# First four attention chunks: loads in order of need, and the next chunk's scores issued ahead of the current chunk's other products

## The chip, the cores and the metric

One core of one Trainium2 chip runs the whole program. The metric is the device time of one execution in microseconds (us). Of the kernel before there are three timed runs, 1011.18, 1013.14 and 1015.83 us; the median is 1013.14 us.

## The reference

Three layers follow one another on B=4 sequences of S=768 tokens with H=8 heads of D=48 channels (model width 384).

```python
# 1. a recurrence over the tokens of each head (state is 48 x 48)
cur   = (u * k_t) outer v_t
y_t   = r_t @ (state + cur)
state = w_t[:, None] * state + k_t outer v_t
# 2. an MLP: x is (3072, 384), w_in (384, 2048), w_out (2048, 384)
h = x @ w_in;  g = where(h > 0, h, exp(min(h, 0)) - 1);  x = g @ w_out
# 3. a second MLP of the same shape with g = h * sigmoid(1.702 h)
```

## The kernel before

**The recurrence by chunks.** The tokens are taken in 24 chunks of 128 (six to a sequence). For chunk c the host lays out `w` (decays), `kr` (keys and queries, 112 partitions, four pairs of heads) and `tok` (128 tokens x r, k, v). The steps, with the engine that does each:

- `decay` (VectorE, L240 to L249): two scans, the running product of w (`e`) and its inverse (`gi`), each in one buffer.
- `queries` (L278, `r` = queries times `e`), `keys` (L270, `kh` = keys times `gi`), `weigh` (L330, L331, q·k·u per token) on GpSimd, unless another engine is named.
- `bonus`: VectorE sums `weigh` per head (L341), then GpSimd multiplies v by the sum (L343, `qv`).
- `block` (ScalarE, L290): copies `r` into the block-diagonal `blk`, one buffer.
- `scores_pe` (TensorE): 4 products of `kh` with `blk` into the PSUM tile `pa`, then 4 transposes of `kh` into `pk`. `scores`: two masked copies of `pa` into the one tile `at` (VectorE, L375), and a copy of `pk` to `kt` (ScalarE, L378).
- `y_pe` (TensorE): `at` times v, and `r` times the state. `y` (VectorE, L397) adds `qv`.
- `state_pe` (TensorE), then `state` (VectorE, L417 to L420): the new state `s`.
- `x_pe` (TensorE): transposes y. `xt` (ScalarE L431, VectorE L432): splits it into a high and a low part, the MLP's input.

**The MLPs.** Tokens are taken in 6 tiles of 512 (4 chunks), the hidden width in 16 slices f. Products are in split precision: w and x each as high and low part, three passes. A slice's weights arrive as int words (`raw`) and are rebuilt by three VectorE operations (L97, then L107 twice: "bits"), split by a ScalarE cast (L132) and a VectorE subtraction (L133: "parts"). A step computes `h` (L143, 9 products), the activation (L154 to L156 in layer 1), its split (L166, L167) and the second product (L174). Steps of layer 1's first tile rebuild the weights of slice j+2 as they go. From chunk 4 on, the recurrence's steps are woven into the MLP's steps.

**What sets the order.** Nothing is reordered: each engine runs its instructions in the order in which the program issues them, and waits are put in for data and for buffers. All loads go through one queue (SyncE). Chunks 0 to 3 have no MLP step to run beside: the function `lead` writes out their order. The changed part of the order is all in `lead`: in the loop over c it issues `y_pe(c)`, `state_pe(c)`, `scores_pe(c+1)` and `x_pe(c)`, prepares `decay`, `keys`, `queries`, `block` of chunk c+2, and takes slices of weight work (`take`) beside them. `warm` issues bf16 products on constant data that nothing reads (L353). At its end the first weight slices are ready, and the MLP starts.

Of the kernel before, what the change touches and what calls it, by code (L numbers as in the profile page):

```python
# [12 lines left out]
F32 = mybir.dt.float32  # L13
# [9 lines left out]
B, H, S, D = 4, 8, 768, 48  # L23
P = 128
C = 128
NCB = S // C
NCH = B * NCB
NP = H // 2
PR = 112
HALF = ((0, 48), (64, 112))  # L30
NT = B * S
DM = H * D
# [19 lines left out]
class Moe:  # L52
# [33 lines left out]
    large = small = None  # L86
# [106 lines left out]
class Attention:  # L193
# [79 lines left out]
    def queries(self, c, engine=None):  # L273
        if c >= NCH or "r" in self.t[c]:
            return
        nc, t = self.nc, self.t[c]
        r = t["r"] = self.p.tile([PR, NP, C], F32, tag="r", name="r", bufs=2)
        (engine or nc.gpsimd).tensor_tensor(out=r, in0=t["kr"][:, NP * C:].rearrange("p (s t) -> p s t", t=C),  # L278
                                            in1=t["e"][:, :, :C], op=ALU.mult)

# [27 lines left out]
    def verdict(self, bad):  # L308

        nc = self.nc  # L310
        large = self.p.tile([P, CHECKS], F32, tag="rk", name="large")
        s = self.p.tile([P, 2], F32, tag="q", name="s")
        nc.vector.tensor_scalar(out=large, in0=self.c["large"], scalar1=HIGH_LARGE, scalar2=0.0,
                                op0=ALU.is_lt, op1=ALU.is_equal)
        nc.vector.tensor_reduce(out=s[:, 0:1], in_=large, axis=AX.X, op=ALU.add)
        nc.vector.tensor_reduce(out=s[:, 1:2], in_=self.c["flag"], axis=AX.X, op=ALU.add)
        pb = self.ps.tile([P, H, C], F32, tag="a", name="pb", bufs=1)[:, 0, :]
        for i in range(2):
            nc.tensor.matmul(pb[:1, :1], self.c["one"], s[:, i:i + 1], start=i == 0, stop=i == 1)
        nc.vector.tensor_scalar(out=bad, in0=pb[:1, :1], scalar1=0.0, scalar2=None, op0=ALU.not_equal)  # L320

    def weigh(self, c, engine=None):

        if c >= NCH or "rk" in self.t[c]:
            return
        nc, t = self.nc, self.t[c]
        tok = t["tok"]
        rk = t["rk"] = self.p.tile([P, DM], F32, tag="rk", name="rk")
        engine = engine or nc.gpsimd
        engine.tensor_tensor(out=rk, in0=tok[:, :DM], in1=tok[:, DM:2 * DM], op=ALU.mult)  # L330
        engine.tensor_tensor(out=rk, in0=rk, in1=self.c["u"], op=ALU.mult)  # L331
# [23 lines left out]
    def scores_pe(self, c):  # L355
        nc, t = self.nc, self.t[c]
        kh, blk = t["kh"], t["blk"]
        pa = t["pa"] = self.ps.tile([P, H, C], F32, tag="a", name="pa", bufs=1)
        if "khl" in t:
            mm = [partial(nc.tensor.matmul, pa[:, 2 * p:2 * p + 2, :], t["khl"][:, a, p, :], blk[:, b, p, :, :],  # L360
                          start=i == 0, stop=i == len(PASSES) - 1) for p in range(NP) for i, (a, b) in enumerate(PASSES)]
        else:
            mm = [partial(nc.tensor.matmul, pa[:, 2 * p:2 * p + 2, :], kh[:, p, :], blk[:, p, :, :],
                          start=True, stop=True) for p in range(NP)]
        if not self.last(c):
            pk = t["pk"] = self.psum("pk")
            mm += [partial(nc.tensor.transpose, pk[:, p * PR:(p + 1) * PR], kh[:, p, :], self.c["ident"][:PR, :PR])
                   for p in range(NP)]
        return mm

    def scores(self, c):
        nc, t, at = self.nc, self.t[c], self.c["at"]
        m = self.c["mask"].unsqueeze(1).to_broadcast([P, NP, C])
        for j in range(2):
            nc.vector.copy_predicated(at[:, NP * j:NP * (j + 1), :], m, t["pa"][:, NP * j:NP * (j + 1), :])  # L375
        if not self.last(c):
            kt = t["kt"] = self.p.tile([P, NP * PR], F32, tag="kt", name="kt", bufs=2)
            nc.scalar.copy(kt, t["pk"][:, :NP * PR])  # L378
# [14 lines left out]

    def y(self, c):
        nc, t = self.nc, self.t[c]
        x = t["x"] = self.p.tile([P, DM], F32, tag="x", name="x")
        nc.vector.tensor_tensor(out=x, in0=t["qv"].rearrange("p h d -> p (h d)"), in1=t["py"][:, :DM], op=ALU.add)  # L397

    def state_pe(self, c):
# [42 lines left out]
def issue(a, b, late=0):  # L442

    for f in a[:late]:
        f()
    a, done = a[late:], 0
    for i, f in enumerate(a):
        f()
        while done < len(b) and (done + 1) * len(a) <= (i + 1) * len(b) + len(a) // 2:
            b[done]()  # L450
            done += 1
    for f in b[done:]:
        f()
# [4 lines left out]
LATE = (0, 6, 2, 6)  # L458


MADE, BITS = (0, 0, 1, 2), (0, 3, 7, 8)
WARM = (11, 4, 2)
AHEAD = MADE[-1]
NTILE = NT // TILE
STEPS = 2 * NTILE * NF
CHECKS = 4 * NF
# [3 lines left out]
def layers(nc, moe, w1, w2, x2d, out, x_of, beside, lead):  # L470
# [66 lines left out]
    for j in range(STEPS):  # L537
# [10 lines left out]
        if j < turn:  # L548
            n = min(j + AHEAD + 1, NF)
            loads, squares, bits = min(n + 3, NF), min(n + 1, NF), 4 * n  # L550
# [70 lines left out]
def fast(tc, rkw, tok, u, w1, w2, out, bad, x2d):  # L621
    nc = tc.nc
    with ExitStack() as ctx:
# [6 lines left out]
        with tc.manual_schedule():  # L630
            moe = Moe(nc, pools, ps)
            c = {}
            at = Attention(nc, ap, c, ps, rkw, tok)
# [8 lines left out]
            per = TILE // C  # L642

            def xt(c):
                i, o = divmod(c, per)
                if i not in xts:
                    xts[i] = pools["xt"].tile([P, 2, KD, TILE], F32R, tag="xt", name="xt")
                at.xt(c, xts[i], o * C)
# [30 lines left out]
            first = 4 * per + 1  # L679

            def lead(take):
                at.load(0)
                at.load(1, 0)
                nc.sync.dma_start(at.c["u"], u.partition_broadcast(P))
                at.load_tok(0)
                at.load(1, 1)
                at.load(2, 0)
                take("load", 1)
                at.load(2, 1)
                at.load_tok(1)  # L690
                at.load_tok(2)
                at.load(3)
                at.load_tok(3)
                take("load", 2)
                at.load(4)
                at.decay(0)
                at.queries(0)
                at.keys(0, nc.vector)
                at.block(0, (nc.scalar.copy, nc.vector.tensor_copy))
                at.warm(WARM[0])  # L700
                issue(at.scores_pe(0), [])
                at.decay(1)
                at.queries(1)
                at.keys(1)
                at.scores(0)
                at.weigh(0, nc.vector)
                at.bonus(0)
                at.block(1)
                for c in range(per):
                    made = MADE[c]  # L710
                    at.warm(WARM[1])
                    issue(at.y_pe(c), [])
                    at.decay(c + 2)
                    at.bonus(c)
                    take("bits", BITS[c])
                    at.keys(c + 2)
                    at.queries(c + 2)
                    at.weigh(c + 1)
                    at.warm(WARM[2])
                    issue(at.state_pe(c), [])  # L720
                    at.y(c)
                    if c == per - 1:
                        issue(at.x_pe(c), [])
                    issue(at.scores_pe(c + 1), [])
                    at.state(c)
                    if c == per - 1:
                        xt(c)
                    at.scores(c + 1)
                    if c < per - 1:
                        issue(at.x_pe(c), [])  # L730
                        xt(c)
                    if c == 0:
                        take("load", 3)
                        at.load_tok(4)
                        at.load(5)
                        at.load_tok(5)
                    take("bits", 4 * made)
                    take("parts", made)
                    at.block(c + 2)
                take("load", 5)  # L740
                at.load(per + 2)
                at.bonus(per)
                at.alone = False

            def beside(j):
# [13 lines left out]
                return ([], 0, lambda: None, decays) if 0 <= k <= NCH and odd else NOTHING  # L759

            layers(nc, moe, w1, w2, x2d, out, xts.pop, beside, lead)


def any_decay(tc, wkr, vrow, up, w1, w2, out, x2d, xd):
# [48 lines left out]
    with ExitStack() as ctx:  # L813
# [12 lines left out]
        def lead(take):  # L826
            for k in range(AHEAD):
                for what, n in (("load", 1), ("sq", 1), ("bits", 4), ("parts", 1)):
                    take(what, n * (k + 1))
            take("load", AHEAD + 3)  # L830
            take("sq", AHEAD + 1)

# [55 lines left out]
```

## Time and profile before

| | |
|---|---|
| median of three runs | 1013.14 us |
| profiled execution: time / span | 1009.45 us / 1007.2 us |
| mean granted TensorE clock | 0.979 |
| busy: TensorE / VectorE / ScalarE / GpSimd | 966.6 / 707.3 / 459.6 / 179.5 us |
| chain that ended last: TensorE / VectorE | 78% / 14% |

The span is the profiled execution from the first to the last instruction; the 2.25 us around it are in the time and not in the span. In the rows further down, PE is TensorE (PEld its weight loads), DVE VectorE, ACT ScalarE, POOL GpSimd and SP SyncE. A timeline row reads: start in us, duration in us, engine, line, operation, out<-in, shapes, count; in brackets the idle time of the engine before it and what ended it. Rows of one line and engine close together are merged. L448 and L450 are the helper through which the products are issued; their tile names tell them apart.

### The profile page before, as it was taken

What the parts mean: (1) busy time and instruction counts of PE and PEld (TensorE: products, weight loads), DVE (VectorE), ACT (ScalarE), POOL (GpSimd) and SP (SyncE); (2) the same over time, 40 slices, a digit from 0 to 9 for tenths busy, and PEclk for the clock granted to TensorE, in tenths of its full rate; (3) what the DMA queues carried; (4) which work ended last, traced back from release to release, by engine and by line L of the source; (5) the groups of instructions that cost most, each with busy time, mean ns of one, the idle gap of its engine ahead of it and who ended that gap; (6) DMA issues with size and microseconds to landing.
All of it is one profiled execution on the core that took longest, in us unless ns stands there. A gap on an engine that the chain in (4) does not pass through costs nothing.

```text
span 1007.2 us, 13002 instructions
## 1 busy us (share of the span) xinstructions
PE 966.6 (96%) x4895; PEld 829.3 (82%) x4895; DVE 707.3 (70%) x1102; ACT 459.6 (46%) x886; POOL 179.5 (18%) x147
## 2 busy tenths in 40 slices
PE   7888889999999999999999999999999999999997
PEld 5677677788888878878888879999989899899896
DVE  7999997677667766776635888757666676676432
ACT  3243344444444445444445554446565565544322
POOL 5542323333323423423300000000000000000000
PEclk9798989999999999999999999999999999999999
DMA  9845401221211222212005560134353354432001
GB/s 239 231 176 177 146 28 51 86 72 52 83 51 51 61 83 71 74 45 90 1 1 193 195 216 25 41 119 135 122 181 123 119 180 124 142 116 79 32 1 35
DMA packets 35351, 101.89 MB, mean 101 GB/s; under 512 B 4048, under 2 KB 7248, under 8 KB 35280
## 3 DMA queue, kind: packets, MB, share of 16 engines
q1 hardware_dynamic: 35280, 100.98, 31.4%
q8 instruction: 40, 0.66, 0.3%
q14 instruction: 31, 0.25, 0.1%
HBM read 91.53 MB, written 9.44 MB: 100 GB/s over the span
## 4 chain that ended last, share of the span: by engine, by line
PE 78%; DVE 14%; issue 3%; POOL 2%; ACT 1%; DMA 0%; ACTq 0%; POOLq 0%; DVEq 0%
PE h L143 34%; PE o L183 20%; PE o L174 16%; DVE wt L107 4%; PE py L450 3%; PE pa L450 2%; DVE w L133 2%; DVE hl L167 1%; DVE wt L97 1%; DVE g L156 1%; PE pd L450 1%; DVE parts L294 1%; DVE e L240 1%; DVE gi L247 1%; ACT w L132 1%
## 5 line engine op out<-in xcount | busy, mean ns | idle before, releaser
L143 PE MATMUL h<-xt,w 128*128 128x512 f32 x1728 | 469.4, 401 | 4.2 <-DVE w L133 3.0
L143 PEld LDWEIGHTS h<-xt,w 128*128 128x128 f32 x1728 | 318.1, 189 | 66.5 <-DVE w L133 5.8
L174 PE MATMUL o<-hl,w 128*128 128x512 f32 x864 | 280.5, 428 | 6.1 <-DVE x L515 6.1
L183 PE MATMUL o<-w,hl 128*128 128x384 f32 x1152 | 217.8, 337 | 3.1 <-ACT e L159 2.1
L183 PEld LDWEIGHTS o<-w,hl 128*128 128x128 f32 x1152 | 204.4, 188 | 13.0 <-ACT e L159 3.3
L166 ACT CAST hl<-g 128x512 fp32r<-128x512 f32 x192 | 118.9, 619 | 188.4 <-DVE g L156 86.0
L174 PEld LDWEIGHTS o<-hl,w 128*128 128x128 f32 x864 | 158.5, 193 | 32.5 <-DVE x L515 7.5
L167 DVE TENSOR_TENSOR hl<-g,hl 128x512 fp32r<-128x512 f32 x192 | 150.2, 783 | 43.7 <-ACT hl L166 42.4
L156 DVE SCALAR_TENSOR_TENSOR g<-e,h 128x512 f32<-128x512 f32 x96 | 65.6, 683 | 68.1 <-ACT e L155 67.7
L160 DVE TENSOR_TENSOR g<-e,h 128x512 f32<-128x512 f32 x96 | 65.9, 686 | 66.5 <-ACT e L159 66.5
L159 ACT ACTIVATE e<-h 128x512 f32<-128x512 f32 x96 | 57.3, 597 | 101.0 <-PE h L143 101.0
L154 ACT ACTIVATE e<-h 128x512 f32<-128x512 f32 x96 | 57.3, 596 | 54.2 <-PE h L143 54.0
L450 PEld LDWEIGHTS py<-tok,at 128*128 128x128 f32 x304 | 60.4, 200 | 15.7 <-issue 4.4
L107 DVE SCALAR_TENSOR_TENSOR wt<-raw,wt 128x768 int32<-128x768 int32 x64 | 67.5, 1055 | 1.6
L155 ACT ACTIVATE e<-e 128x512 f32<-128x512 f32 x96 | 60.7, 632 | 3.1
L375 DVE COPY_PREDICATED at<-mask,pa 128x512 f32<-128x512 int32 x48 | 32.3, 726 | 38.6 <-PE pa L450 38.5
L270 POOL TENSOR_TENSOR kh<-kr,gi 112x512 f32<-112x512 f32 x19 | 31.6, 1661 | 150.1 <-issue 133.0
L450 PE MATMUL py<-tok,at 128*128 128x48 f32 x304 | 50.3, 248 | 6.2 <-issue 3.6
L450 PE MATMUL pa<-parts,khl 112*128 112x256 f32 x192 | 54.5, 284 | 1.0 <-DVE parts L294 1.0
L123 DVE TENSOR_SCALAR checked<-checked 128x384 f32<-128x384 f32 x64 | 22.8, 356 | 39.7 <-ACT checked L122 39.7
L378 ACT COPY kt<-pk 128x448 f32<-128x448 f32 x20 | 10.7, 534 | 86.2 <-PE pk L450 64.0
L132 ACT CAST w<-wt 128x768 fp32r<-128x768 f32 x32 | 26.7, 833 | 49.5 <-DVE wt L107 44.5
(111 smaller groups left out, 933.4 us busy)
## 6 DMA issues: line engine op xcount, KB each, us to landing
raw<-in_w SPq DMA_DIRECT2D x32, 768.0 KB, 4.5
seen<-in_w SPq DMA_DIRECT2D x64, 384.0 KB, 3.2
tok<-in_tok SPq DMA_DIRECT2D x20, 576.0 KB, 3.9
kr<-in_rkw SPq DMA_DIRECT2D x20, 448.0 KB, 3.6
seen<-in_rkw SPq DMA_DIRECT2D x24, 226.2 KB, 3.6
x2d<-x SPq DMA_DIRECT2D x18, 256.0 KB, 2.3
x<-x2d SPq DMA_DIRECT2D x18, 256.0 KB, 3.8
w<-in_rkw SPq DMA_DIRECT2D x20, 226.2 KB, 2.6
```

The costliest lines, as they stand in the source:

```text
L107: yield nc.vector.scalar_tensor_tensor(out=ti, in0=a, scalar=n, in1=ti, op0=shift, op1=put)
L143: nc.tensor.matmul(h[:, :n], w[:, a, k * P:(k + 1) * P], x[:, b, k, :n], start=i == 0, stop=i == len(mm) - 1)
L154: nc.scalar.activation(e[:, :n], h[:, :n], AF.Exp)
L155: nc.scalar.activation(e[:, :n], e[:, :n], AF.Relu, bias=1.0, scale=-1.0)
L156: nc.vector.scalar_tensor_tensor(out=g[:, :n], in0=e[:, :n], scalar=-1.0, in1=h[:, :n], op0=ALU.mult, op1=ALU.max)
L159: nc.scalar.activation(e[:, :n], h[:, :n], AF.Sigmoid, scale=1.702)
L160: nc.vector.tensor_tensor(out=g[:, :n], in0=e[:, :n], in1=h[:, :n], op=ALU.mult)
L166: nc.scalar.copy(hl[:, 0, :n], g[:, :n])
L167: nc.vector.tensor_tensor(out=hl[:, 1, :n], in0=g[:, :n], in1=hl[:, 0, :n].bitcast(F32), op=ALU.subtract)
L174: nc.tensor.matmul(acc[d][:, :n], w[:, a, DM + d * P:DM + (d + 1) * P], hl[:, b, :n], start=f == 0 and i == 0, stop=f == NF - 1 and i == 2)
L183: nc.tensor.matmul(acc[s][:, :DM], hl[:, b, s * P:(s + 1) * P], w[:, a, DM:2 * DM], start=f == 0 and i == 0, stop=f == NF - 1 and i == 2)
L450: b[done]()
```

## The change

The loads of chunks 0 to 2 come chunk by chunk. In the loop, `scores_pe(c+1)` is issued first, then `x_pe(c-1)`, `y_pe(c)`, `state_pe(c)`. So that scores of two chunks can be live at once, odd chunks put theirs into the two PSUM banks of tag `h`, and a third `r` buffer is added. `rk` (the result of `weigh`) and `x` lie in `tok` instead of tiles of their own. `queries(0)` moves from GpSimd to VectorE. The `warm` products in the loop are gone (those ahead of it stay). On VectorE, `xt` of the chunk before stands after `bonus`, the masked copies of the next chunk stand before `state`, and the weight work of `take` stands behind `block`, at c=2 and c=3 alone.

```diff
-        rk = t["rk"] = self.p.tile([P, DM], F32, tag="rk", name="rk")
+        rk = t["rk"] = tok[:, DM:2 * DM]
...
-        pa = t["pa"] = self.ps.tile([P, H, C], F32, tag="a", name="pa", bufs=1)
+        if self.alone and c % 2:
+            pa = [self.ps.tile([P, NP, C], F32, tag="h", name="pa", bufs=2) for _ in range(2)]
+        else:
+            pa = self.ps.tile([P, H, C], F32, tag="a", name="pa", bufs=1)
+            pa = [pa[:, :NP, :], pa[:, NP:, :]]
...
-        x = t["x"] = self.p.tile([P, DM], F32, tag="x", name="x")
+        x = t["x"] = t["tok"][:, :DM]
...
-MADE, BITS = (0, 0, 1, 2), (0, 3, 7, 8)
-WARM = (11, 4, 2)
+BITS = (0, 0, 4, 8)
+WARM = 11
...
             def lead(take):
-                at.load(0)
-                at.load(1, 0)
-                nc.sync.dma_start(at.c["u"], u.partition_broadcast(P))
-                at.load_tok(0)
-                at.load(1, 1)
-                at.load(2, 0)
+                for c in range(3):
+                    at.load(c)
+                    at.load_tok(c)
+                    if c == 0:
+                        nc.sync.dma_start(at.c["u"], u.partition_broadcast(P))
                 take("load", 1)
-                at.load(2, 1)
-                at.load_tok(1)
-                at.load_tok(2)
                 at.load(3)
...
-                at.queries(0)
+                at.queries(0, nc.vector)
...
                 at.scores(0)
+                at.block(1)
                 at.weigh(0, nc.vector)
-                at.bonus(0)
-                at.block(1)
                 for c in range(per):
-                    made = MADE[c]
-                    at.warm(WARM[1])
+                    issue(at.scores_pe(c + 1), [])
+                    if c > 0:
+                        issue(at.x_pe(c - 1), [])
                     issue(at.y_pe(c), [])
+                    issue(at.state_pe(c), [])
                     at.decay(c + 2)
                     at.bonus(c)
-                    take("bits", BITS[c])
+                    if c > 0:
+                        xt(c - 1)
                     at.keys(c + 2)
                     at.queries(c + 2)
                     at.weigh(c + 1)
-                    at.warm(WARM[2])
-                    issue(at.state_pe(c), [])
                     at.y(c)
-                    if c == per - 1:
-                        issue(at.x_pe(c), [])
-                    issue(at.scores_pe(c + 1), [])
+                    at.scores(c + 1)
                     at.state(c)
-                    if c == per - 1:
-                        xt(c)
-                    at.scores(c + 1)
-                    if c < per - 1:
-                        issue(at.x_pe(c), [])
-                        xt(c)
                     if c == 0:
+                        at.load_tok(4)
                         take("load", 3)
-                        at.load_tok(4)
                         at.load(5)
                         at.load_tok(5)
-                    take("bits", 4 * made)
-                    take("parts", made)
                     at.block(c + 2)
+                    take("bits", BITS[c])
+                    take("parts", BITS[c] // 4)
+                issue(at.x_pe(c), [])
+                xt(c)
                 take("load", 5)
                 at.load(per + 2)
                 at.bonus(per)
```

## Rows read from the trace of the kernel before

**Rows 1.** Windows of all engines: stretch, busy us of each, PEclk, DMA share, GB/s.

```profile
25.00:58.00 33.00, 27.34 (x148) 22.73 (x146) 31.13 (x51) 8.11 (x14) 19.16 (x15) 0.79 0.73 207
58.00:160.00 102.00, 89.11 (x405) 70.62 (x404) 100.08 (x134) 40.68 (x68) 29.97 (x19) 0.92 0.36 126
160.00:300.00 140.00, 137.70 (x746) 116.10 (x745) 98.10 (x145) 62.06 (x108) 46.91 (x37) 1.00 0.21 67
```

**Rows 2.** Timeline of VectorE, the decays of chunks 3, 4, 5 and one sum.

```profile
24.86 1.23 DVE L240 TENSOR_TENSOR_SCAN e<-lent,sep 112x516 f32<-112x516 f32 x1 [2.19 <-DMA lent<-in_rkw]
...
27.82 0.55 DVE L341 TENSOR_REDUCE q<-rk 128x8 f32<-128x384 f32 x1
...
34.57 1.32 DVE L240 TENSOR_TENSOR_SCAN e<-lent,sep 112x516 f32<-112x516 f32 x1
...
46.95 1.22 DVE L240 TENSOR_TENSOR_SCAN e<-w,sep 112x516 f32<-112x516 f32 x1
```

**Rows 3.** Issue to landing: decays of chunk 1 (issued 1.74 us), then tok 0 (2.69).

```profile
DMA to landing us min/median/max: 5.3/5.3/5.3
...
DMA to landing us min/median/max: 9.0/9.0/9.0
```

**Rows 4.** Timeline of TensorE: a `y_pe`; scores to transposes of one turn.

```profile
21.68 1.99 PE L448 MATMUL py<-lent,at 128*128 128x48 f32 x16
...
23.50 1.10 PE L448 MATMUL py<-s,r 112*128 112x96 f32 x8
...
40.99 1.92 PE L448 MATMUL pa<-x,kh 112*128 112x256 f32 x8
...
43.13 0.49 PE L448 MATMUL px<-ident,x 128*128 128x128 f32 x3
```

**Rows 5.** Timeline of GpSimd and ScalarE: `kh`, `r`, `block`, `qv`.

```profile
19.69 1.18 POOL L270 TENSOR_TENSOR kh<-lent,gi 112x512 f32<-112x512 f32 x1 [1.71 <-DVE sep L249]
...
20.83 1.18 POOL L278 TENSOR_TENSOR r<-lent,e 112x512 f32<-112x512 f32 x1
...
22.05 1.26 ACT L290 COPY x<-r 48x512 f32<-48x512 f32 x2 [0.70 <-POOL r L278]
...
28.44 1.07 POOL L343 TENSOR_TENSOR lent<-lent,q 128x384 f32<-128x384 f32 x1 [4.37 <-DVE q L341]
```

**Rows 6.** Timeline of VectorE: from `y` over `state` to the masked copies.

```profile
41.92 0.54 DVE L397 TENSOR_TENSOR x<-lent,py 128x384 f32<-128x384 f32 x1
...
44.38 1.34 DVE L375 COPY_PREDICATED at<-mask,pa 128x512 f32<-128x512 int32 x2
```

**Rows 7.** Groups of VectorE, 24.8 to 57.8 us: busy us, mean ns, idle before.

```profile
L107 DVE SCALAR_TENSOR_TENSOR wt<-raw,wt 128x768 int32<-128x768 int32 x4 | 5.2, 1298 | 0.1
...
L432 DVE TENSOR_TENSOR xt<-px,xt 128x384 fp32r<-128x384 f32 x3 | 1.6, 541 | 0.0
```

**Rows 8.** Timeline: three operations of "bits" after the lead, GpSimd idle.

```profile
76.55 0.55 DVE L97 TENSOR_SCALAR wt<-raw 128x768 int32<-128x768 int32 x1
77.13 1.95 DVE L107 SCALAR_TENSOR_TENSOR wt<-raw,wt 128x768 int32<-128x768 int32 x2
```

**Rows 9.** Timeline around the first MLP step.

```profile
55.07 1.87 PE L143 MATMUL h<-xt,w 128*128 128x512 f32 x7
...
55.89 0.84 ACT L132 CAST w<-wt 128x768 fp32r<-128x768 f32 x1
...
56.76 0.96 DVE L133 TENSOR_TENSOR w<-wt,w 128x768 fp32r<-128x768 f32 x1 [0.29 <-ACT w L132]
...
59.23 0.60 ACT L154 ACTIVATE e<-h 128x512 f32<-128x512 f32 x1 [1.34 <-PE h L143]
...
61.76 0.68 DVE L156 SCALAR_TENSOR_TENSOR g<-e,h 128x512 f32<-128x512 f32 x1
```

**Rows 10.** Windows of all engines, a TensorE gap and what follows.

```profile
28.00:30.50 2.50, 0.00 (x0) 0.00 (x0) 2.47 (x4) 0.51 (x1) 2.06 (x2) 1.00 1.04 225
30.50:40.70 10.20, 9.64 (x39) 7.72 (x40) 9.90 (x17) 1.71 (x3) 6.67 (x6) 0.50 1.03 265
```

More of the change, by code (lines that the diff above doesn't have):

```diff
@@ L276, in queries @@
         nc, t = self.nc, self.t[c]
-        r = t["r"] = self.p.tile([PR, NP, C], F32, tag="r", name="r", bufs=2)
+        r = t["r"] = self.p.tile([PR, NP, C], F32, tag="r", name="r", bufs=3)
         (engine or nc.gpsimd).tensor_tensor(out=r, in0=t["kr"][:, NP * C:].rearrange("p (s t) -> p s t", t=C),
@@ L310, in verdict @@
         nc = self.nc
-        large = self.p.tile([P, CHECKS], F32, tag="rk", name="large")
+        large = self.p.tile([P, CHECKS], F32, tag="kt", name="large", bufs=2)
         s = self.p.tile([P, 2], F32, tag="q", name="s")
@@ L357, in scores_pe @@
         kh, blk = t["kh"], t["blk"]
-        pa = t["pa"] = self.ps.tile([P, H, C], F32, tag="a", name="pa", bufs=1)
+        if self.alone and c % 2:
[3 more added lines that the diff above has]
+            pa = [pa[:, :NP, :], pa[:, NP:, :]]
+        t["pa"] = pa
+        of = lambda p: pa[2 * p // NP][:, 2 * p % NP:2 * p % NP + 2, :]
         if "khl" in t:
-            mm = [partial(nc.tensor.matmul, pa[:, 2 * p:2 * p + 2, :], t["khl"][:, a, p, :], blk[:, b, p, :, :],
+            mm = [partial(nc.tensor.matmul, of(p), t["khl"][:, a, p, :], blk[:, b, p, :, :],
                           start=i == 0, stop=i == len(PASSES) - 1) for p in range(NP) for i, (a, b) in enumerate(PASSES)]
         else:
-            mm = [partial(nc.tensor.matmul, pa[:, 2 * p:2 * p + 2, :], kh[:, p, :], blk[:, p, :, :],
+            mm = [partial(nc.tensor.matmul, of(p), kh[:, p, :], blk[:, p, :, :],
                           start=True, stop=True) for p in range(NP)]
@@ L374, in scores @@
         for j in range(2):
-            nc.vector.copy_predicated(at[:, NP * j:NP * (j + 1), :], m, t["pa"][:, NP * j:NP * (j + 1), :])
+            nc.vector.copy_predicated(at[:, NP * j:NP * (j + 1), :], m, t["pa"][j])
         if not self.last(c):
@@ L458 @@
 LATE = (0, 6, 2, 6)
-MADE, BITS = (0, 0, 1, 2), (0, 3, 7, 8)
-WARM = (11, 4, 2)
-AHEAD = MADE[-1]
+BITS = (0, 0, 4, 8)
+WARM = 11
+AHEAD = BITS[-1] // 4
 NTILE = NT // TILE
@@ L696, in lead @@
                 at.decay(0)
-                at.queries(0)
+                at.queries(0, nc.vector)
                 at.keys(0, nc.vector)
                 at.block(0, (nc.scalar.copy, nc.vector.tensor_copy))
-                at.warm(WARM[0])
+                at.warm(WARM)
                 issue(at.scores_pe(0), [])
```

## The prediction

> **What bounds the kernel now.** I read the windows of all engines by stage first. From 160 us on TensorE is busy in 137.70 of 140 us [rows 1]: nothing in `lead` changes that stage, so the change can only move its beginning. From 58 to 160 us VectorE is busy in 100.08 of 102 us (it rebuilds layer 1's weights), and from 25 to 58 us, the second half of the lead, in 31.13 of 33 us [rows 1]. VectorE is thus the bound from 25 to 160 us, and whatever it loses there, waiting or working longer, shifts the rest. Next I read the timeline for what VectorE can't get round. The decay of chunk 3 starts at 24.86 us, after 2.19 us of idle ended by a load [rows 2]: there the lead is set by the loads. The lead ends for TensorE with the first MLP product at 55.07 us and for VectorE with the last "parts" at 56.76 + 0.96 = 57.7 us; VectorE's first activation operation (L156) starts at 61.76 us [rows 9], and from there on its work is the same before and after. So the question is when that L156 starts in the changed kernel.
>
> **Up to the third decay: nothing.** Decays 1 land at 1.74 + 5.3 = 7.0 us, tok 0 at 2.69 + 9.0 = 11.7 us [rows 3]. In the new order tok 0 and `u` stand ahead of decays 1, so these land when the same bytes are through, near 11.7 us. VectorE then does decay 1 (3.0 us: 24.86 to 27.82 [rows 2]) to 14.7, the copies of chunk 0 (1.34 [rows 6]) to 16.0, `weigh(0)` (two operations of about 0.55, by the 0.54 of rows 6) to 17.1, decay 2 and its sum (3.5, with the 0.55 [rows 2]) to 20.6. GpSimd's `qv`, `kh` and `r` [rows 5] end 3.5 us later, at 24.1; meanwhile VectorE ends `y(0)`, copies and a two-operation `state` at some 24.5. The loads ahead of decays 3 are the same set as before (chunks 0 to 2, `u`, one weight slice), so they land at the same 24.8 us. Both kernels start decay 3 there: early gains or losses up to some 2 us are swallowed by that load.
>
> **The parts of a turn.** Decay and sum 3.5 us [rows 2]. `qv` 1.1, `kh` and `r` 2.4, so `r` ends 3.5 us after the sum; `block` 1.26 [rows 5]. Scores, `pk` and transposes 40.99 to 43.62 = 2.65 us; `y_pe` 21.68 to 24.60 = 2.9 us [rows 4]. `y`, `state` and the masked copies 41.92 to 45.72 = 3.8 us [rows 6]. `xt` 0.54 [rows 7]. The three "bits" operations 0.55 + 1.95 = 2.5 us alone [rows 8]; in the lead L107 has a mean of 1.30 us against 0.98 [rows 7, 8], because GpSimd works beside it, so 2.5 to 3.5. I take 2.5: in the new order they come when GpSimd's turn is nearly over. "Parts" is 0.84 on ScalarE, then 0.96 on VectorE [rows 9].
>
> **Turn c=1.** Decay 3 and the sum run from 24.9 to 28.4. On TensorE `scores_pe(2)` now stands ahead of `y_pe(1)`. It needs `block(2)`, thus `r(2)`, which ends at about 24.1: start 25.4, scores and transposes to 28.0, `y_pe(1)` to 30.95. VectorE has only `xt(0)` in hand, so it waits 2.0 us; in the kernel before it did "bits" there. `y(1)`, copies and `state(1)` end at 34.75. Before, decay 4 started at 34.57 [rows 2], with one "bits" pair and one `xt` (2.0 us of work) already behind it.
>
> **Turn c=2.** Decay 4 and the sum to 38.25; `qv(2)` to 39.35. TensorE: `r(3)` ends at 31.9, `block(3)` 33.15, scores and transposes 35.8, `y_pe(2)` 38.7, hidden. VectorE: `xt(1)`, 0.55 of waiting for `qv`, the block of 3.8 to 43.15, "bits" to 45.65, then it waits 0.84 for ScalarE's cast, and "parts" to 47.45. Decay 5 started at 46.95 before [rows 2].
>
> **Turn c=3.** Decay 5 and the sum to 50.95; `qv(3)` to 52.05; `y(3)`, copies, `state` to 55.85; "bits" 58.35; cast 59.2; "parts" 60.15; `xt(3)` 60.7. Here the change moves the weight work of slice 1 ahead of `xt(3)` and so ahead of the first product: before, `xt(3)` stood in front of "parts". First product 60.7 against 55.07, VectorE's lead done at 60.7 against 57.7.
>
> **The first step.** From the first product to the first exponential takes 59.23 - 55.07 = 4.16 us, and to the end of the two ScalarE operations 1.25 more [rows 9]. L156 at 66.15 against 61.76: +4.4 us. Between, VectorE has a sum and one "bits" (some 3 us) and waits for the rest.
>
> **The clock.** TensorE did nothing from 28 to 30.5 us, and in the 10.2 us after that its granted clock was 0.50, that is 1.2 of 2.4 GHz [rows 10]. In the new order it has nothing from `x_pe(3)` (about 53.2) to 60.7, and the constant products that would fill such gaps are dropped. So the first step runs at least partly at 1.2 GHz: between 0 and 4.2 us more, I take 2.5. A second gap, of some 3 us ahead of `scores_pe(2)`, can slow the 5.55 us of scores, transposes and `y_pe(1)`, which in turn c=1 are on the path: 0 to 5, I take 1.5. In turns 2 and 3 `y_pe` has 0.6 and 3 us to spare. The Trainium skill ("TensorE: Matmul & The Clock Gate", section "What's actually happening") has throttled as the default state and activity as what releases it; the trace agrees with 0.50 after the gap, and the rule speaks against dropping the constant products.
>
> **GpSimd beside VectorE.** If "bits" do meet `weigh`, 2 x (3.5 - 2.5) = 2 us more; that is in the upper end of the range. The Trainium skill ("SBUF — State Buffer", section "SBUF: two separate sides") calls the ports that the two engines share an exclusive lock, the loser waiting for a whole instruction; L107's 1.30 against 0.98 us agrees in kind, and by the rule the sum would lie nearer this upper end.
>
> **What costs nothing.** `queries(0)` on VectorE delays `keys(0)` by less than the GpSimd operation that it had to share with. `rk` and `x` inside `tok` keep `tok` until `x_pe`, one MLP step longer, and the loads behind it on the queue with it; the DMA share of 0.36 in 58 to 160 us [rows 1] leaves room for that. If it did not, a weight slice would be late and VectorE would wait on a load. The third `r` buffer and the PSUM banks of tag `h` are free in the lead.
>
> **The sum.** 4.4 + 2.5 + 1.5 = +8.4 us. Against the profiled execution's own 1009.45 us (span 1007.2) that is 1017.9; it lies 3.7 us under the median of the timed runs, so the prediction is made from the median: 1013.1 + 8.4 = 1021.5, rounded 1021.
>
> **Rivals.**
> *The clock stays up.* Then only the order counts: +4.4, 1017.5. For it: the first gap may be filled by slower early products. Against: the gap of 7.5 us.
> *TensorE at 1.2 GHz through the lead.* Without the constant products the turn's chain of scores, transposes and `y_pe` takes up to twice 5.55 us and becomes the bound: `y(1)` at some 36, `y(3)` near 60, the first product near 69, its step doubled: about +16, 1029. For it: in 30.5 to 40.7 us the clock stayed low although TensorE was busy for 9.64 of 10.2 us [rows 10]. Against: mean clock 0.79 in the second half even before [rows 1], mostly hidden.
> *Not slower: the scores ahead pay.* If VectorE never waits for TensorE or ScalarE, the 2.0 us of c=1, twice 0.84 and the waits for `qv` (1.1) fall out: first product at 55.9, L156 at 61.4. With fewer meetings of L107 and GpSimd (some 0.3 us each on four) the result is -0.4 to -2, about 1011.5. It decides if decay 5 starts before 46.95 less the 2 us of work it is behind, about 45. Much below that the load at 24.8 us and VectorE's 31.13 us of work behind it [rows 1] don't allow.
>
> **Chances.** The forecast (+5.5 to +12, that is 1018.6 to 1025) 0.38; clock stays up 0.28; clock low throughout 0.17; not slower 0.17. A difference of 0.5%, 5.07 us, is about what a measurement of this kernel tells from none. Slower by more: the forecast, 0.05 of the second case and the third, 0.60. Faster by more: 0.08, half of the last case, for what I have not seen. Within: 0.32. The range runs from 1011, under the last case's time, to 1030, over the third's.
>
> **What would show it.** Decay 3 at 24.8 us with an idle time ended by a load; a wait of VectorE for `y_pe(1)` near 28 to 31 us; decay 5 near 47.5; the order cast, "parts", `xt(3)` ahead of the first product at about 61; granted clock 0.50 at that product; L156 near 69. It is wrong if decay 5 starts well before 46 us, if the decay of chunk 3 doesn't wait for its load, or if the shift at L156 is not found again at the end, because the stage up to 160 us gives it back.

## The result, and the profile after

The changed kernel takes 1022.3 us (median, 1021.72 to 1022.72) against 1012.16 us for the kernel before in the same comparison: the medians lie 10.1 us apart, and the ratio of the means is 1.0093, 95% interval 1.0066 to 1.012. It is slower, by 9.4 us by that ratio. The prediction was 1021 us, range 1011 to 1030. The profiled execution after took 1022.17 us with a span of 1020.4 us, 12.7 us more than the profiled execution before. That one, 1009.45 us, is among the shortest of its kernel (medians of 1010.97 to 1014.74 us in the comparisons further down), so shifts against its profile are rather too large than too small.

The same stages as [rows 1], after the change:

```profile
25.00:58.00 33.00, 22.49 (x144) 20.22 (x144) 27.39 (x48) 7.27 (x13) 16.88 (x16) 0.83 0.60 179
58.00:160.00 102.00, 89.25 (x381) 71.77 (x382) 94.18 (x124) 37.27 (x61) 25.08 (x16) 0.84 0.35 123
160.00:300.00 140.00, 136.10 (x718) 114.19 (x718) 98.34 (x145) 61.11 (x107) 47.21 (x36) 0.98 0.21 65
```

VectorE was busy in 31.13 of the 33 us up to 58 us; now it is in 27.39. It waits, and part of the work comes later. Where it waits stands in its timeline after the change (the decays of chunks 3, 4 and 5 answer to [rows 2]):

```profile
24.43 1.24 DVE L240 TENSOR_TENSOR_SCAN e<-lent,sep 112x516 f32<-112x516 f32 x1
...
28.09 0.55 DVE L341 TENSOR_REDUCE q<-lent 128x8 f32<-128x384 f32 x1
...
29.56 0.56 DVE L438 TENSOR_TENSOR xt<-px,xt 128x384 fp32r<-128x384 f32 x1 [0.93 <-ACT xt L437]
...
32.17 0.56 DVE L403 TENSOR_TENSOR lent<-lent,py 128x384 f32<-128x384 f32 x1 [2.04 <-PE py L454]
...
35.38 1.23 DVE L240 TENSOR_TENSOR_SCAN e<-lent,sep 112x516 f32<-112x516 f32 x1
...
43.47 1.24 DVE L97 TENSOR_SCALAR wt<-raw 128x768 int32<-128x768 int32 x1
...
47.60 0.96 DVE L133 TENSOR_TENSOR w<-wt,w 128x768 fp32r<-128x768 f32 x1 [0.90 <-ACT w L132]
...
48.48 1.23 DVE L240 TENSOR_TENSOR_SCAN e<-w,sep 112x516 f32<-112x516 f32 x1
```

In turn c=1 it stands for 0.93 + 2.04 us behind TensorE's products, in turn c=2 for 0.90 us behind ScalarE's cast. The end of the lead answers to [rows 9], with all engines:

```profile
59.81 0.83 ACT L132 CAST w<-wt 128x768 fp32r<-128x768 f32 x1 [3.28 <-DVE wt L107]
60.55 0.47 ACT L437 CAST xt<-px 128x384 fp32r<-128x384 f32 x1
60.67 0.96 DVE L133 TENSOR_TENSOR w<-wt,w 128x768 fp32r<-128x768 f32 x1 [0.90 <-ACT w L132]
61.07 0.80 PE L143 MATMUL h<-xt,w 128*128 128x512 f32 x1 [6.57 <-ACT xt L437]
61.66 0.56 DVE L438 TENSOR_TENSOR xt<-px,xt 128x384 fp32r<-128x384 f32 x1
...
62.27 2.92 PE L143 MATMUL h<-xt,w 128*128 128x512 f32 x6 [0.41 <-DVE xt L438]
...
69.50 0.60 ACT L154 ACTIVATE e<-h 128x512 f32<-128x512 f32 x1 [8.48 <-PE h L143]
...
70.79 0.69 DVE L156 SCALAR_TENSOR_TENSOR g<-e,h 128x512 f32<-128x512 f32 x1 [4.47 <-ACT e L155]
```

The order is cast, "parts" (L133), then `xt(3)` (L437, L438). The first product starts at 61.07 us instead of 55.07, and from there to the first exponential it takes 8.43 us instead of 4.16. L156 starts at 70.79 instead of 61.76 us: +9.0. TensorE's gap ahead of that product and the stretch behind it, as windows:

```profile
54.50:61.00 6.50, 0.01 (x1) 0.00 (x0) 5.42 (x9) 2.42 (x4) 2.79 (x3) 0.50 0.75 240
61.00:74.00 13.00, 12.52 (x43) 10.71 (x44) 8.40 (x12) 2.58 (x5) 4.35 (x3) 0.50 0.49 204
```

The granted clock (PEclk, as in [rows 1]) is 0.50, 1.2 GHz, over the whole first step.

Set L156 of one kernel beside L156 of the other, step by step: +9.0 at step 0, +9.9 at step 1, and +9.9 at every step to 14. Then +11.4 at step 15 and +12.95 at step 19, where it stays. The last 3.05 us are two falls of the clock, at 169.7 and 193.6 us. The first, as a window of the changed kernel, then a window of the kernel before around the same work:

```profile
169.70:173.00 3.30, 3.30 (x12) 2.81 (x11) 1.50 (x3) 0.62 (x1) 1.21 (x1) 0.50 0.00 0
```

```profile
157.00:161.50 4.50, 3.37 (x17) 2.84 (x18) 4.24 (x7) 0.62 (x1) 0.65 (x1) 1.00 0.00 0
```

The work there is the same in both kernels.

### The profile page after: what moved, and what is told of

Its sections match the earlier page's. It is cut to its first block, busy times and chain, and to the rows that moved or that the text cites. A ratio compares the mean times of both kernels' runs of the same rounds, so it can differ in the third digit from the quotient of the medians.

```text
span 1020.4 us, 12970 instructions
## 1 busy us (share of the span) xinstructions
PE 968.9 (95%) x4871; PEld 833.4 (82%) x4871; DVE 706.0 (69%) x1103; ACT 459.8 (45%) x886; POOL 174.0 (17%) x146
## 4 chain that ended last, share of the span: by engine, by line
PE 77%; DVE 13%; issue 4%; ACT 2%; POOL 2%; DMA 1%; SPq 0%; ACTq 0%; POOLq 0%
PE h L143 34%; PE o L183 20%; PE o L174 15%; PE py L456 3%; DVE wt L107 3%; PE pa L456 2%; DVE w L133 2%; DVE hl L167 1%; DVE wt L97 1%; DVE g L156 1%; PE pd L456 1%; DMA lent<-in_rkw 1%; DVE parts L294 1%; ACT w L132 1%; ACT hl L166 1%
## 5 line engine op out<-in xcount | busy, mean ns | idle before, releaser
L143 PE MATMUL h<-xt,w 128*128 128x512 f32 x1728 | 474.6, 404 | 9.5 <-ACT xt L437 6.6
L156 DVE SCALAR_TENSOR_TENSOR g<-e,h 128x512 f32<-128x512 f32 x96 | 65.6, 684 | 73.2 <-ACT e L155 72.9
L456 PEld LDWEIGHTS py<-tok,at 128*128 128x128 f32 x304 | 60.9, 201 | 15.4 <-issue 4.4
L155 ACT ACTIVATE e<-e 128x512 f32<-128x512 f32 x96 | 60.7, 632 | 3.1
```

The costliest lines, as they stand in the source:

```text
L143: nc.tensor.matmul(h[:, :n], w[:, a, k * P:(k + 1) * P], x[:, b, k, :n], start=i == 0, stop=i == len(mm) - 1)
L155: nc.scalar.activation(e[:, :n], e[:, :n], AF.Relu, bias=1.0, scale=-1.0)
L156: nc.vector.scalar_tensor_tensor(out=g[:, :n], in0=e[:, :n], scalar=-1.0, in1=h[:, :n], op0=ALU.mult, op1=ALU.max)
```

## The experiments

Each kernel was compared with the kernel before on the same chip. The times of one kernel's executions spread over up to some 10 us, so the first L156 of its profile is the finer measure; where VectorE waits for ScalarE's second activation (L155) ahead of it, L156 less that wait tells when VectorE itself was ready. "Before" and "after" are the two kernels. The columns from "decay 3" to "first exponential" and "L156" are starts in us, the wait is in us.

One profile is one execution, and it carries accidents of its own. After, e1, e2 and e8 run the same code up to decay 4, yet decay 3 starts between 24.23 and 25.87 us in them. Decay 4 starts between 35.38 and 35.77: `y(1)` has to wait for `y_pe(1)`, and that swallows most of the difference. Profile and times need not agree either: the profiled execution of e12 takes 6.1 us more than that of before, while its ratio is 1.0007.

| kernel | decay 3 | first product | first exponential | wait at L156 | L156 | ratio to before (95%) |
|---|---|---|---|---|---|---|
| before | 24.86 | 55.07 | 59.23 | 0 | 61.76 | |
| after | 24.43 | 61.07 | 69.50 | 4.47 | 70.79 | 1.0093 (1.0066, 1.012) |
| e1 | 25.87 | 57.39 | 63.88 | 0 | 66.28 | 1.0032 (1.0003, 1.0061) |
| e2 | 25.79 | 61.32 | 68.05 | 2.77 | 69.35 | 1.0067 (1.0037, 1.0097) |
| e3 | 23.64 | 56.14 | 60.30 | 0 | 62.85 | 0.9986 (0.9958, 1.0013) |
| e4 | 24.02 | 55.10 | 59.23 | 0 | 61.81 | 1.0001 (0.9973, 1.0028) |
| e5 | 26.47 | 60.04 | 68.48 | 4.48 | 69.77 | 1.0095 (1.0058, 1.0133) |
| e6 | 23.85 | 59.42 | 67.86 | 4.47 | 69.15 | 1.0063 (1.0036, 1.009) |
| e7 | 26.04 | 58.85 | 65.14 | 1.44 | 66.44 | 1.0022 (0.9994, 1.0049) |
| e8 | 24.23 | 63.93 | 68.09 | 2.64 | 69.38 | 1.0063 (1.0037, 1.0088) |
| e9 | 26.10 | 62.19 | 70.01 | 4.47 | 71.30 | 1.0099 (1.0066, 1.0131) |
| e10 | 23.77 | 55.75 | 61.40 | 0 | 64.63 | 1.0019 (0.9996, 1.0041) |
| e11 | 23.23 | 56.27 | 62.44 | 1.48 | 63.73 | 1.0027 (1.0, 1.0053) |
| e12 | 23.61 | 57.55 | 65.37 | 3.22 | 66.66 | 1.0007 (0.998, 1.0034) |

**e1: after, with `xt(3)` ahead of the weight work.**

```diff
                     at.block(c + 2)
+                    if c == per - 1:
+                        issue(at.x_pe(c), [])
+                        xt(c)
                     take("bits", BITS[c])
                     take("parts", BITS[c] // 4)
-                issue(at.x_pe(c), [])
-                xt(c)
```

> The changed kernel, but at c=3 the transposes x_pe(3) and the split xt(3) are issued ahead of that turn's weight work (bits and parts of slice 1). Theory (the order of the lead's weight work is part of the loss): xt(3) ends near 57 us, the first MLP product starts there instead of 61.1 us, and the first L156 comes about 4 us earlier than the 70.8 us of the changed kernel, near 67; the end moves by as much. Rival (only the low TensorE clock of the first step and the later turns cost time, VectorE's total work is the same): the first L156 stays within 1 us of 70.8.

Measured, the first step of e1:

```profile
57.39 3.52 PE L143 MATMUL h<-xt,w 128*128 128x512 f32 x7 [2.94 <-ACT xt L437]
...
63.88 0.60 ACT L154 ACTIVATE e<-h 128x512 f32<-128x512 f32 x1 [2.64 <-PE h L143]
...
66.28 0.68 DVE L156 SCALAR_TENSOR_TENSOR g<-e,h 128x512 f32<-128x512 f32 x1
```

L156 comes 4.5 us earlier than in after and waits for nothing: it now stands behind VectorE's own work. Half of the 9.0 us was the place of `xt(3)`, with what the late step added by its clock; 4.5 us are left, and they are VectorE's. Decay 4 starts 0.3 us later than in after, so the gain does not come from the early part.

**e9: before, with the weight work ahead of `xt(3)`.** The counter-test: nothing else of the change is in it.

```diff
-                    take("bits", BITS[c])
+                    take("bits", (0, 3, 4, 4)[c])
...
-                    if c == per - 1:
-                        issue(at.x_pe(c), [])
                     issue(at.scores_pe(c + 1), [])
                     at.state(c)
-                    if c == per - 1:
-                        xt(c)
...
                     take("bits", 4 * made)
                     take("parts", made)
                     at.block(c + 2)
+                issue(at.x_pe(c), [])
+                xt(c)
```

> The kernel before with x_pe(3) and xt(3) moved behind the turn's weight work, and the bits of slice 1 all in turn c=3 (counts 0, 3, 4, 4 with the rest behind the state), as the changed kernel has it; everything else as before. Theory (weight work ahead of xt(3) delays the first product): first product near 58.8 us instead of 55.1, granted clock 0.50 there after the gap, first L156 between 64 and 68 us instead of 61.8. Rival (VectorE does the same work in another order, so nothing is lost): within 1 us of 61.8.

Measured, the first step of e9, and the gap and the step as windows:

```profile
62.17 0.56 DVE L432 TENSOR_TENSOR xt<-px,xt 128x384 fp32r<-128x384 f32 x1 [0.70 <-ACT xt L431]
...
62.19 3.52 PE L143 MATMUL h<-xt,w 128*128 128x512 f32 x7 [8.34 <-ACT xt L431]
...
70.01 0.60 ACT L154 ACTIVATE e<-h 128x512 f32<-128x512 f32 x1 [7.88 <-PE h L143]
71.30 0.69 DVE L156 SCALAR_TENSOR_TENSOR g<-e,h 128x512 f32<-128x512 f32 x1 [4.47 <-ACT e L155]
```

```profile
54.00:62.00 8.00, 0.00 (x0) 0.00 (x0) 6.43 (x9) 2.31 (x4) 3.13 (x3) 0.73 0.76 256
62.00:74.00 12.00, 11.81 (x40) 10.21 (x41) 7.29 (x10) 2.70 (x5) 4.35 (x3) 0.50 0.43 179
```

This edit alone gives nearly the whole loss: L156 at 71.30 us, 3.3 us past the range expected, ratio 1.0099. Of the 9.5 us at L156 up to 1.25 are not the edit's: up to decay 4 the code is that of before, and decay 3 started at 26.10 instead of 24.86 us because its load landed later, decay 4 at 35.82 instead of 34.57. The edit makes a gap of 8.3 us on TensorE, and the step behind the gap runs at 0.50, although the constant products of the loop are all there.

**e2 and e8: after, with constant products in the gap.** 22 in e2, 36 in e8.

```diff
                 issue(at.x_pe(c), [])
+                at.warm(22)
                 xt(c)
```

> The changed kernel with 22 constant products (as in warm) issued behind x_pe(3), in TensorE's gap of 6.6 us ahead of the first MLP product. Theory (the first step is slow because the granted clock is 0.50 there): clock 1.00 at the first product, the step from first product to first exponential takes 4.2 us instead of 8.4, and the first L156 comes near 66.5 us instead of 70.8, 4.3 us earlier. Rival (the step is long because of the woven y_pe(4) and its waits, not the clock): within 1 us of 70.8.

> As the kernel with 22 constant products behind x_pe(3), but 36, so that they end only when xt(3) does, at about 62.5 us. Theory (with 22 the clock fell again because they ended at 59.1 us and the first products waited for xt(3) until 62.5): granted clock 1.00 from 62.5 us on, the woven first step takes no more than 4.5 us, the first L156 comes near 67.5 us, 3.3 us earlier than in the changed kernel. Rival (the clock of the first step does not matter): no earlier than the 69.35 us with 22.

Measured, first the windows of e2, then the window and the first step of e8:

```profile
57.70:62.70 5.00, 2.11 (x9) 0.82 (x8) 4.00 (x6) 1.21 (x2) 0.00 (x0) 1.00 1.01 384
62.80:66.10 3.30, 3.30 (x12) 2.71 (x11) 3.23 (x4) 0.00 (x0) 3.02 (x3) 0.50 1.02 425
```

```profile
57.60:72.00 14.40, 14.40 (x82) 9.86 (x81) 10.70 (x14) 4.09 (x7) 4.54 (x4) 1.00 0.72 279
```

```profile
63.93 1.86 PE L143 MATMUL h<-xt,w 128*128 128x512 f32 x7
...
68.09 0.60 ACT L154 ACTIVATE e<-h 128x512 f32<-128x512 f32 x1 [6.66 <-PE h L143]
...
69.38 0.69 DVE L156 SCALAR_TENSOR_TENSOR g<-e,h 128x512 f32<-128x512 f32 x1 [2.64 <-ACT e L155]
```

Both missed the gain expected, each for another reason. In e2 the constant products end at 59.13 us, and after another 2.2 us of nothing the first product starts at 61.32; the clock falls within the step. In e8 the clock stays at 1.00 and the step takes 68.09 - 63.93 = 4.16 us, to the digit that of the kernel before; but 36 products last until 63.93, though `xt(3)` is done at 62.63, and push the step back. That the low clock doubles the step is shown; what exactly it costs in after is not. An estimate: at 1.00 the products from 62.27 on would reach the exponential 3.8 us later (as 55.39 to 59.23 in the kernel before), and L156 would start at 67.4: 3.4 of the 9.0 us.

**e3: before, without the constant products in the loop.**

```diff
-                    at.warm(WARM[1])
...
-                    at.warm(WARM[2])
```

> The kernel before without the constant products inside the loop (4 and 2 per turn); the 11 ahead of the loop stay. Theory (TensorE is hidden behind VectorE in most turns, so a low clock in the lead costs little until a turn waits for y_pe): first L156 between 61.8 and 65 us, against 61.76. Rival (dropping them is the main cause of the change's loss): first L156 near 70, +8 us.

L156 at 62.85: +1.1, and a ratio of 0.9986 whose interval contains 1. The rival falls. Past step 14 this profile gains the same 3.05 us as after (L156 +1.1 at step 14, +4.1 at step 19), with the clock at 0.50 as well:

```profile
161.10:164.40 3.30, 3.30 (x12) 2.81 (x11) 1.28 (x3) 0.46 (x1) 1.15 (x1) 0.50 0.00 0
```

So do e2, e5, e8 and e9. Before, e1, e4, e6, e7, e11 and e12 have neither fall, and e10 has the first alone. The work there is the same in all of them, so these 3 us belong to no one edit; what decides about them is not shown.

**e4: before, with the new order of the first loads alone.** The `load` lines of the change ahead of the loop, nothing else.

> The kernel before with the changed order of the first loads alone. Theory (the early part is swallowed): decay 1 starts about 2 us later, near 10.9 us; the load of chunk 3's decays lands near 22.6 us as in the changed kernel, so decay 3 starts at 23 to 24.9 us, and the first L156 is 0 to 2 us earlier than 61.76. Rival (the new order of loads is itself the loss): first L156 2 us later or more.

Decay 1 started at 11.02 us, decay 3 at 24.02, L156 at 61.81. The order of the first loads neither gains nor costs.

**e5: after, with the bits behind `bonus`.**

```diff
                     at.bonus(c)
+                    take("bits", (0, 3, 7, 8)[c])
                     if c > 0:
                         xt(c - 1)
...
-                    take("bits", BITS[c])
-                    take("parts", BITS[c] // 4)
+                    take("bits", 4 * (0, 0, 1, 2)[c])
+                    take("parts", (0, 0, 1, 2)[c])
```

> The changed kernel with the bits of the weight work taken right behind bonus, 3 at c=1, 4 at c=2, 1 at c=3, as in the kernel before; parts stay behind block. Theory (VectorE waits 2 us for y_pe(1) with nothing in hand, and at c=3 three bits operations stand ahead of xt(3)): the wait is filled, one bits operation is left ahead of xt(3), the first product comes near 58.6 us instead of 61.1, the first L156 2 to 3 us earlier than 70.8. Rival (collisions of bits with GpSimd's qv, keys and queries eat the gain): less than 1 us earlier.

Only 1.0 us earlier. But the profile lost 2.0 us ahead of turn c=1, where both kernels have the same code: VectorE waited 3.67 us for `y_pe(0)` (1.56 in after), and decay 3 started at 26.47 instead of 24.43.

```profile
24.03 0.55 DVE L403 TENSOR_TENSOR tok<-tok,py 128x384 f32<-128x384 f32 x1 [3.67 <-PE py L454]
...
26.47 1.23 DVE L240 TENSOR_TENSOR_SCAN e<-lent,sep 112x516 f32<-112x516 f32 x1
```

From decay 3 to L156 it is 43.3 us against 46.4. That does not make 3 us of gain: e12, further down, starts decay 3 2.4 us earlier than the kernel it is compared with and decay 4 only 0.1. What the bits' place is worth stays inconclusive.

**e6: after, with the scores behind the current chunk's products again.**

```diff
-                    issue(at.scores_pe(c + 1), [])
                     if c > 0:
                         issue(at.x_pe(c - 1), [])
                     issue(at.y_pe(c), [])
                     issue(at.state_pe(c), [])
+                    issue(at.scores_pe(c + 1), [])
```

> The changed kernel with scores_pe(c+1) issued behind x_pe(c-1), y_pe(c) and state_pe(c) again; banks, loads, weight work as changed. Theory (scores ahead cost y(1) 2 us of waiting at c=1): y(1) no longer waits for TensorE, decay 4 starts 1 to 2 us earlier than 35.4 us, and the first L156 1 to 2 us earlier than 70.8. Rival (scores ahead pay, as the change means them to): decay 4 and the first L156 later by 1 us or more.

`y(1)` starts at 29.19 us instead of 32.17 and waits for GpSimd's `qv` (0.35) alone:

```profile
29.19 0.56 DVE L403 TENSOR_TENSOR lent<-lent,py 128x384 f32<-128x384 f32 x1 [0.35 <-POOL lent L343]
...
32.76 1.92 DVE L240 TENSOR_TENSOR_SCAN e<-lent,sep 112x516 f32<-112x516 f32 x1
```

Decay 4 is 2.6 us earlier, L156 1.6. In this order, issuing the scores ahead costs time. One of the 2.6 us is gone by decay 5 (46.83 against 48.48 us): the first scan of decay 4 alone took 1.92 us here and 1.23 in after. The first step still starts late and runs at 0.50, and L156 waits 4.47 us as in after.

**e7, e10, e11: the edits together.** e7 is e1 and e5, e10 is e1 and e6, e11 all three.

> The changed kernel with two edits: xt(3) ahead of the weight work at c=3 (which alone gave a first L156 at 66.3 us), and the bits taken right behind bonus (which alone gave 69.8 instead of 70.8). Theory (what is left of the loss after xt(3) is weight work that VectorE could have done while it waited for TensorE): first L156 1 to 2.5 us earlier than 66.3, near 64.5. Rival (the bits in the early turns only push the later turns, as the small gain alone suggests): 66 us or later.

> The changed kernel with xt(3) ahead of the weight work at c=3 and with scores_pe(c+1) behind y_pe(c) and state_pe(c) again (alone: first L156 at 69.2 us instead of 70.8). Theory (the order on TensorE costs VectorE 1.6 us and adds to the order of the weight work): first L156 near 64.7 us. Rival (the two do not add, the clock of the first step decides): 66 us or later.

> The changed kernel with all three edits: xt(3) ahead of the weight work, bits behind bonus, scores_pe(c+1) behind the current chunk's products. Theory (these three make up the loss; loads in order of need, rk and x in tok, banks and dropped constant products do not): first L156 between 61.5 and 63.5 us and the time within 0.3% of the kernel before. Rival (one of the parts left in costs time too): first L156 at 65 us or later.

e10 came out as expected (64.63), e11 0.2 us past its range (63.73, 2.0 us behind before; ratio 1.0027), e7 as its rival had it (66.44). The three edits make up 7 of the 9.0 us. The window of e11's first step:

```profile
56.20:62.50 6.30, 5.83 (x28) 4.74 (x29) 5.95 (x7) 0.92 (x3) 4.01 (x4) 0.73 1.01 378
```

VectorE was ready there at 63.73 - 1.48 = 62.25 us, 0.5 later than in before. The rest of e11's 2.0 us is the first step again: its first product starts 1.2 us later than in before, and it takes 62.44 - 56.27 = 6.17 us instead of 4.16 at a mean clock of 0.73.

**e12: e7, with 8 constant products in TensorE's early gap.**

```diff
                 issue(at.scores_pe(0), [])
+                at.warm(8)
                 at.decay(1)
```

> The kernel with xt(3) ahead of the weight work and the bits behind bonus (first L156 at 66.4 us, decay 3 at 26.0 us, granted clock 0.50 from 8 to 26 us), plus 8 constant products behind scores_pe(0), in TensorE's early gap of 2.5 us. Theory (the low clock of the first 26 us makes y(0) and y(1) wait for y_pe and hides what the bits gain): granted clock 1.00 over most of 16 to 26 us, decay 3 at 24.5 us or earlier, first L156 at 64.5 us or earlier. Rival (decay 3 is held by loads and GpSimd, the early clock is hidden): decay 3 at 25.5 us or later, first L156 within 0.7 us of 66.4.

The windows of e7, then of e12, and the first step of e12:

```profile
16.10:26.00 9.90, 9.90 (x39) 8.89 (x39) 6.00 (x12) 1.77 (x3) 5.07 (x5) 0.50 1.03 322
```

```profile
16.10:26.00 9.90, 5.94 (x39) 5.38 (x40) 8.63 (x15) 1.76 (x3) 5.61 (x5) 0.84 1.03 324
```

```profile
65.37 0.60 ACT L154 ACTIVATE e<-h 128x512 f32<-128x512 f32 x1 [7.02 <-PE h L143]
66.66 0.69 DVE L156 SCALAR_TENSOR_TENSOR g<-e,h 128x512 f32<-128x512 f32 x1 [3.22 <-ACT e L155]
```

Half right. Decay 3 went from 26.04 to 23.61 us, so the early clock had held it. But decay 4 went only from 36.06 to 35.95: a wait in between swallowed the gain. L156 did not move: VectorE was ready at 66.66 - 3.22 = 63.4 us, 1.6 earlier than in e7, and then waited for a first step that ran at 0.50 throughout. One step on, e12 is behind: its L156 comes 6.0 us after that of before, that of e7 4.7 us.

None of the twelve is faster than the kernel before beyond its interval, and none points to a version that would be.

## Why the prediction was right

The sum was +8.4 us, and 9.4 were measured. The order of the lead is shown to be the cause, but that the sum comes so near is partly luck: two of its terms are off in opposite directions. With its 1.5 us for the clock of turn c=1, it has the first product at 62.2 us and the first exponential 6.66 us later; measured are 61.07 and 8.43 us. That is 1.1 us too much for the late start and 1.8 too little for the first step. (Its 66.15 us for L156 is 66.11 by its own terms, which changes nothing.) By its own steps:

- **VectorE is the bound to 160 us, and L156 is where to read the shift: right.** +9.9 from step 1 on, handed through to step 14 without loss. The 3.05 us that the profile adds after that lie beyond 160 us in after, where the sum has nothing. They are falls of the clock that e3 has as well; the profile of before, itself among the shortest, has none.
- **Decay 3 waits for its load at 24.8 us: wrong, and named in the prediction as a sign of being wrong.** The load landed at 9.95 + 12.7 = 22.65 us; I had taken the landing of the kernel before (9.36 + 15.4 = 24.76), since the same bytes stand ahead of it. VectorE came to decay 3 at 24.43 by its own work, 0.4 us from the forecast. That is luck: with the same code up to there, decay 3 started up to 26.47 us (e5). It had little effect, because what swallows early differences is the wait for `y_pe(1)`, not the load. e4 shows the earlier landing in the order of before: no wait for that load, and L156 0.05 us off.
- **Turn c=1: right, the clock's 1.5 us included.** A wait of 2.0 us and 1.5 for the clock were forecast, 0.93 + 2.04 measured. From the scores to `y_pe(1)` TensorE took 25.07 to 32.06 = 6.99 us against the 5.55 added up, +1.4; the mean granted clock from 25 to 29 us was 0.66. e6 takes the scores from ahead of `y_pe(1)`, and the wait for TensorE is gone.
- **Waits for the cast and for `qv`: right.** 0.90 twice against 0.84, 0.35 twice against 0.55. All waits of VectorE from decay 3 to L133 of the second slice add up to 5.5 us in after and 1.0 in before (0.72 and 0.29): the difference is the 4.5 us by which VectorE is late at L156 (66.3 against 61.8). Its earlier decay 3 (0.4 us) and its slower work (0.5 us) cancel.
- **"Bits" alone: the term was low.** L97 took 1.24 instead of 0.55 us in both turns, beside GpSimd's `weigh`; I had taken the lower end. The first starts at 43.47 us, and GpSimd's L331 runs from 43.30 to 44.29. By the Trainium skill ("SBUF — State Buffer", section "SBUF: two separate sides") the ports the two share are held for a whole instruction; L97 agrees with that in kind, ending 0.42 us after L331 in both turns. Decay 5 at 48.48 against 47.45 is this and turn c=1's clock.
- **The weight work ahead of `xt(3)`: right, and the largest part.** First product 61.07 against 60.7 forecast without the clock; e1 undoes it (-4.5 us at L156), e9 does it alone (+9.5, of which up to 1.25 are its late load).
- **The clock of the first step: right in kind, mis-sized.** 2.5 us taken out of a range of 0 to 4.2, 4.27 measured for the step (8.43 against 4.16): the clock was low over all of it, not partly. The step runs at 0.50 behind a gap of 6.57 us and at 1.00 if constant products fill it (e8). The Trainium skill ("TensorE: Matmul & The Clock Gate", section "What's actually happening") has throttled as the default state and activity as what releases it, and both rows agree. The constant products that the change drops are not the main cause, though: dropping them alone costs 1.1 us at L156 (e3), and e9 keeps them and has the slow step. It is the gap.
- **The rivals.** That the clock stays up is ruled out by the 0.50. That TensorE at 1.2 GHz bounds the whole lead is ruled out by the granted clock of after, 0.83 from 25 to 58 us, and its first product at 61 instead of 69 us; e3 says the same of the order before. That scores ahead pay is ruled out by the 2.04 us of waiting and by e6.

What stays open: how the 9.0 us divide between late start and clock to better than the estimate of 3.4, and what lowers the clock in e11's first step. `rk` and `x` in `tok`, the PSUM banks, the third `r` buffer and `queries(0)` on VectorE have no run of their own; e11 has them all, with the dropped constant products, and is 2.0 us behind at L156.

## What to carry to other kernels

Ahead of a stage's first matrix product, issue what that product needs before work that only the second one needs: the engines work in order, so TensorE stands idle until it comes, and here the gap was paid twice, once as lateness and once as a slow clock behind it. Issuing a product early is a cost when its input is late, for it holds the ready products queued behind it. Where a small edit is judged by one profile, read it at a fixed mark, take off the wait there, and check an earlier mark where both kernels run the same code. A difference at the early mark counts only if no wait behind it swallows it.

## What the runs showed of the hardware

The early part of the lead is the same code in after, e1, e2, e5, e7 and e8, yet the granted clock from 16.1 to 26 us was 0.83 in after, 0.67 in e8 and 0.50 in the others. Decay 3 started at 24.43 us in after, at 24.23 in e8 and between 25.79 and 26.47 in the others. The same holds further on: TensorE has gaps of about 1.0, 0.6 and 1.9 us between 156 and 193 us in before and in after alike, and behind them the clock stayed at 1.00 in before and fell to 0.50 twice in after, 1.5 us each time. An integer TENSOR_SCALAR of 128x768 on VectorE took 1.24 us beside GpSimd, 0.55 alone.
